# Attention and Fourier mixing on one core: block-diagonal omega and v, the maximum as bias of exp, a shorter weight narrowing, and a list of matmuls that counts other engines

## The chip, the cores and the metric

The kernel runs on one core of one Trainium2 chip. The metric is the device time of one execution in microseconds (us); a median over the runs is quoted. Engines are named as in the profile: PE is TensorE (PEld its weight loads), DVE is VectorE, ACT is ScalarE, POOL is GpSimd, SP is SyncE. The granted clock is the share of TensorE's full clock rate that the profile's records show for a stretch. PSUM is the memory that matmuls write to; a PSUM slot is one of the few buffers there that a matmul group needs before it can start.

## The reference, cut to what matters

```python
# q, k, v: (8, 8, 576, 64), omega: (128, 64), w1: (512, 2048), w2: (2048, 512), float64 weights
def phi(x):                                   # features of keys and of queries (cut: both are first scaled by 64**-0.25)
    proj = einsum('bhsd,md->bhsm', x, omega)
    h = proj - sum(x*x)/2
    h = h - max(h, axis=-1)
    return exp(h) / sqrt(m)
kv  = einsum('bhsm,bhsd->bhmd', k_p, v);  z = sum(k_p, axis=2)
att = (q_p @ kv) / (q_p @ z + 1e-6)           # -> x: (batch 8, 576, 512)
X = fft(fft(x, axis=1), axis=2);  u = x + real(X)          # mixing, one per batch
un = (u - mean) / sqrt(var + 1e-6)
out = u + relu(un @ w1) @ w2                               # the MLP
```

The weights come as 64-bit floats and the chip works in 32 bits, so the kernel narrows both weight matrices itself, with integer operations on the high and low words. A **pair** below is two heads of one batch: four pairs make a batch and there are 32. A batch can be mixed when its four pairs are done. The MLP needs the mixed rows and the narrowed weights. TensorE's matmuls go by the names of their outputs: `tps` and `tp` are transposes, `pp` the features, `kvp` and `ndp` the two products of attention, `yp` and `ab` the two of mixing, `hp` and `op` the two layers of the MLP.

## The kernel before: the parts concerned

Narrowing one part (256 columns): a load, seven operations on VectorE, an addition on GpSimd.

```python
def narrow(dst, src):
    raw = cvt.tile([128, n, 2], U32, name="raw", tag="raw")
    nc.gpsimd.dma_start(raw, src)
    lo, hi = raw[:, :, 0], raw[:, :, 1]
    nc.vector.tensor_scalar(ta[:], hi, 0x7FFFFFFF, None, op0=ALU.bitwise_and)
    nc.vector.tensor_scalar(ta, ta, HI_LOW, HI_HIGH, op0=ALU.max, op1=ALU.min)   # the clamp
    # ... (cut: four more bit operations) ...
    nc.vector.scalar_tensor_tensor(rest[:], lo, 2.0**-52, tb[:].bitcast(F32), ...)
    nc.gpsimd.tensor_tensor(out=dst, in0=ta[:].bitcast(F32), in1=rest[:], op=ALU.add)
```

The features of a pair (`pp`), with both heads in the two halves of the array's rows:

```python
for t in range(3):
    for j in range(3):
        for par in range(2):
            rows = slice(D * par, D * par + D)               # 64 of 128 rows
            nc.tensor.matmul(ps[:, par, MF*j : MF*j+MF], lhsT=kqT[rows, 3*t+j, :], rhs=omT[rows, :])
    nc.vector.tensor_reduce(mx[:], pr4, axis=AX.X, op=ALU.max)
    nc.vector.tensor_tensor(out=e, in0=pr4, in1=mx(broadcast), op=ALU.subtract)
    nc.scalar.activation(out=e[:], in_=e[:], func=AF.Exp, scale=SCALE)
```

Mixing of a batch: three gathers by GpSimd, `half` and `fold` on VectorE and GpSimd, then matmuls `yp` and `ab`.

```python
def mix(b):
    nc.sync.dma_start(x[0:CW, 0:NC3, :], rows[...])              # xs, written by the batch's four pairs
    for c in range(NC3):                                         # NC3 = 3
        nc.gpsimd.indirect_dma_start(out=x[:, NC3 + c, :], in_=rows[:, :], in_offset=turned[:, c])
    yield 0.0, 5.0
    # ... (cut: half and fold, first on VectorE, then on GpSimd) ...
    yield 0.0, 6.0
    for n, tab in enumerate((cs, cs, sn, sn)):
        # ... (cut: yp <- fold, tab; y <- yp) ...
        yield 1.5, (11.0 if n == 1 else 1.0)
```

TensorE's order is made when the program is built: every stream of work (weights, mixing, two of pairs, the MLP) gives, at each `yield`, the time on TensorE of what it has just issued and the time until it can go on, and the loop takes the stream that is ready first. These times are constants in the code; nothing at run time changes the order. The order of the other engines' instructions is settled when the program is built too, around TensorE's; in the trace of the kernel after, the 260 operations and transfers of GpSimd stand in just the built order.

Of the kernel before, what the change touches and what calls it, by code (L numbers as in the profile page):

```python
# [12 lines left out]
AF = mybir.ActivationFunctionType  # L13
# [15 lines left out]


HI_LOW = float(np.uint32(896 << 20).view(np.float32))
# [31 lines left out]
def kernel(  # L63
# [24 lines left out]
    CV = 256  # L88
# [3 lines left out]
    TB = 512  # L92
    NTB = B * S // TB
    SCALE = 1.0 / math.sqrt(math.sqrt(D))
# [6 lines left out]
    ld = ctx.enter_context(tc.tile_pool(name="ld", bufs=2))  # L101
    att = ctx.enter_context(tc.tile_pool(name="att", bufs=2))
    fft = ctx.enter_context(tc.tile_pool(name="fft", bufs=1))
    small = ctx.enter_context(tc.tile_pool(name="small", bufs=4))
    cvt = ctx.enter_context(tc.tile_pool(name="cvt", bufs=2))
# [23 lines left out]

    def load_v(n):  # L130
        b, pr = divmod(n, NP)
        h = slice(2 * pr, 2 * pr + 2)
        v1 = ld.tile([P, R, D + 1], F32, name="v1", tag="v1")
        nc.sync.dma_start(v1[:, :, 0:D], v[b, h].rearrange("i (p r) d -> (i p) r d", r=R))
        nc.gpsimd.memset(v1[:, :, D : D + 1], 1.0)  # L135
        loaded["v", n] = v1

    om = const.tile([128, 2, D], F32, name="om")
    for i in range(2):
        nc.sync.dma_start(om[:, i, :], omega[:, :])  # L140
    for n in range(2):
        load(n)
        load_v(n)
# [26 lines left out]
    def narrow(dst, src):  # L170


        n = dst.shape[1]
        raw = cvt.tile([128, n, 2], U32, name="raw", tag="raw")
        nc.gpsimd.dma_start(raw[:].rearrange("p n two -> p (n two)"), src.bitcast(U32))
        lo, hi = raw[:, :, 0], raw[:, :, 1]
        ta = cvt.tile([128, n], U32, name="ta", tag="ta", bufs=1)
        tb = cvt.tile([128, n], U32, name="tb", tag="tb", bufs=1)

        nc.vector.tensor_scalar(ta[:], hi, 0x7FFFFFFF, None, op0=ALU.bitwise_and)  # L180
        nc.vector.tensor_scalar(
            ta[:].bitcast(F32), ta[:].bitcast(F32), HI_LOW, HI_HIGH, op0=ALU.max, op1=ALU.min
        )

        nc.vector.tensor_scalar(
            ta[:], ta[:], 3, 0x40000000, op0=ALU.logical_shift_left, op1=ALU.bitwise_xor
        )
        nc.vector.tensor_scalar(tb[:], hi, 0x80000000, None, op0=ALU.bitwise_and)
        nc.vector.scalar_tensor_tensor(
            ta[:], ta[:], 0x7FFFFFFF, tb[:], op0=ALU.bitwise_and, op1=ALU.bitwise_or  # L190
        )
        nc.vector.tensor_scalar(tb[:], ta[:], 0xFF800000, None, op0=ALU.bitwise_and)
        rest = cvt.tile([128, n], F32, name="rest", tag="rest", bufs=1)
        nc.vector.scalar_tensor_tensor(  # L194
            rest[:], lo, 2.0**-52, tb[:].bitcast(F32), op0=ALU.mult, op1=ALU.mult
        )
        nc.gpsimd.tensor_tensor(out=dst, in0=ta[:].bitcast(F32), in1=rest[:], op=ALU.add)  # L197
# [4 lines left out]
    def weights():  # L202
        for f in range(0, DFF, CV):
            for j in range(NDC):
                dst, src = w1[:, j, f : f + CV], w1v[:, j, f : f + CV]
                if src.dtype == F32:
                    nc.gpsimd.dma_start(dst, src)
                else:
                    narrow(dst, src)
                    yield 0.0, 3.0  # L210
            there["w1"] = f + CV
        for j in range(NFC):
            for f in range(0, DM, CV):
                dst, src = w2[:, j, f : f + CV], w2v[:, j, f : f + CV]
                if src.dtype == F32:
                    nc.gpsimd.dma_start(dst, src)
                else:
                    narrow(dst, src)
                    yield 0.0, 3.0
            there["w2"] = j + 1  # L220


    omT = const.tile([128, MF], F32, name="omT")
    omps = sml_tile("omps")
    nc.tensor.transpose(omps[:, 0:128], om[:].rearrange("m i d -> m (i d)"), ident[:])
    nc.vector.tensor_copy(out=omT[:], in_=omps[:, 0:128])
# [4 lines left out]

# [23 lines left out]
    def attn(n):  # L255
        b, pr = divmod(n, NP)
        kq, v1 = loaded.pop(n), loaded.pop(("v", n))
# [3 lines left out]
        if n + 2 < B * NP:  # L261
            load(n + 2)
        yield 1.0, 2.2
# [3 lines left out]
        for t in range(3):  # L267
            ps = big_tile("pp")
            for j in range(3):
                for par in range(2):  # L270
                    rows = slice(D * par, D * par + D)
                    nc.tensor.matmul(  # L272
                        ps[:, par, MF * j : MF * j + MF],
                        lhsT=kqT[rows, 3 * t + j, :],
                        rhs=omT[rows, :],
                    )
            pr4 = ps[:, :, 0:384].rearrange("p two (c m) -> p two c m", m=MF)
            mx = small.tile([P, 2, 3], F32, name="mx", tag="mx")
            nc.vector.tensor_reduce(mx[:], pr4, axis=AX.X, op=ALU.max)  # L279
            e = att.tile([P, 6, MF], F32, name="e", tag="e", bufs=6)  # L280
            nc.vector.tensor_tensor(  # L281
                out=e[:].rearrange("p (c two) m -> p two c m", two=2),
                in0=pr4,
                in1=mx[:].unsqueeze(3).to_broadcast([P, 2, 3, MF]),
                op=ALU.subtract,
            )
            nc.scalar.activation(out=e[:], in_=e[:], func=AF.Exp, scale=SCALE)  # L287
            es.append(e)
            if t:
                yield (1.0, 2.5) if t == 1 else (0.7, 2.5)  # L290

        def feature(c):
            return es[c // 6][:, c % 6, :]

        kvp = big_tile("kvp")
        for r in range(R):
            for i in range(2):
                rows = slice(D * i, D * i + D)
                nc.tensor.matmul(  # L299
                    kvp[:, i, 0 : D + 1],  # L300
                    lhsT=feature(r)[rows],
                    rhs=v1[rows, r, :],
                    start=(r == 0),
                    stop=(r == R - 1),
                )
        kv = att.tile([128, 2, D + 1], F32, name="kv", tag="kv")
        nc.vector.tensor_copy(out=kv[:], in_=kvp[:, :, 0 : D + 1])
        if n + 2 < B * NP:
            load_v(n + 2)
        yield 2.3, 0.5  # L310
        qeT = transposed(lambda r: feature(R + r), "qeT")
        yield 1.0, 2.2
# [31 lines left out]
        yield 1.4, 0.0  # L344


    def mix(b):
        NR = 2 * NC3
        x = fft.tile([CP, NR, DM], F32, name="x", tag="x")
# [12 lines left out]
        yield 0.0, 5.0  # L362
# [25 lines left out]
        yield 0.0, 6.0  # L388

        y = fft.tile([128, 4, NK], F32, name="y", tag="y")  # L390
        for n, tab in enumerate((cs, cs, sn, sn)):
            yp = sml_tile("yp")
            for c in range(NC3):
                nc.tensor.matmul(  # L394
                    yp[:, 0:NK],
                    lhsT=fold[:, c, n, :],
                    rhs=tab[:, c, :],
                    start=(c == 0),
                    stop=(c == NC3 - 1),
                )  # L400
            nc.scalar.activation(out=y[:, n, :], in_=yp[:, 0:NK], func=AF.Copy)
            yield 1.5, (11.0 if n == 1 else 1.0)
        for c in range(NC3):

            ab = big_tile("ab")
# [15 lines left out]
            bmp = fft.tile([CP, 3, KD + 1], F32, name="bmp", tag="fold")  # L421
# [11 lines left out]
            for g, (left, right) in enumerate(((mi, pl), (pl, mi))):  # L433
                u = x[:, NC3 * g + c, :]
                nc.gpsimd.tensor_tensor(  # L435
                    out=u[:, 0:KD], in0=u[:, 0:KD], in1=left[:, 0:KD], op=ALU.add
                )
                nc.gpsimd.tensor_tensor(
# [12 lines left out]
            yield 1.4, 2.0  # L451
        done["mix"] = b + 1
# [14 lines left out]
    def prep(j):  # L467
        while done.get("first", 0) < j:
            yield None
        unT = mlpp.tile([128, NDC, TB], F32, name="unT", tag="unT", bufs=1)  # L470
        for i in range(TB // 128):
            t = TB // 128 * j + i
            u = mlpp.tile([P, DM], F32, name="u", tag="u", bufs=2)
            for p, b, s in rows_of(t):
                nc.sync.dma_start(u[p], us[b][s, :])
            st = small.tile([P, 6], F32, name="st", tag="st")
# [9 lines left out]
            yield 0.0, (6.0 if i == 0 else 1.5)  # L486
# [10 lines left out]
            yield 0.5, 0.5  # L497
        uns[j] = unT
        done["prep"] = j + 1
# [4 lines left out]
    def mlp(j):  # L504
        unT = uns.pop(j)
        hs = []
        for fc in range(NFC):
            while there["w1"] < 128 * fc + 128:
                yield None
# [17 lines left out]
            yield 3.45, 0.0  # L527
        for i in range(TB // 128):
            t = TB // 128 * j + i
            ur = mlpp.tile([P, DM], F32, name="ur", tag="ur", bufs=2)  # L530
            for p, b, s in rows_of(t):
                nc.sync.dma_start(ur[p], us[b][s, :])
            yp = mmp.tile([128, DM], F32, name="op", tag="mm")
            for fc in range(NFC):
                while there["w2"] < fc + 1:
                    yield None
                nc.tensor.matmul(  # L537
                    yp[:],
                    lhsT=hs[fc][:, 128 * i : 128 * i + 128],
                    rhs=w2[:, fc, :],  # L540
                    start=(fc == 0),
                    stop=(fc == NFC - 1),
# [80 lines left out]
```

## Time and profile before

The time is 1615.7 us (1611.88 to 1616.73). The profiled span is 1612.1 us.

| | before |
|---|---|
| PE busy | 1430.2 us |
| DVE, ACT, POOL busy | 562.8, 243.2, 304.3 us |
| mean granted clock of TensorE | 0.926 |
| first MLP matmul (`hp`) starts | 187.0 us |
| first gather of mixing issued | 82.8 us |

"Full-clock work" is the sum of TensorE's instructions in the order in which they are listed, each at the rate that it shows in dense stretches at granted clock 1; the prediction shows how the rates are read. "Lost" is the span less that work, and so takes in pauses and time at a lower clock. Before, the work is 1348.8 us and 263.3 are lost: 111.7 by the first `hp` (187.0 us, 75.3 of work listed ahead of it) and 151.6 after it.

### The profile page before, as it was taken

How to read it: one execution, taken by the hardware profiler on the slowest of the kernel's cores; microseconds unless marked ns; L12 is line 12 of the kernel's file. 1: busy time of each engine (PE TensorE's matmuls, PEld its weight loads, DVE VectorE, ACT ScalarE, POOL GpSimd, SP SyncE). 2: the span in 40 equal slices, each digit the busy share in tenths (PEclk: the TensorE clock that was granted, in tenths of full speed). 3: DMA queues.
4: the chain of work that ended last, by engine and by line, in shares of the span. 5: the costliest groups of instructions: out<-in, count | busy, mean ns of one | idle time of the engine just before them, and what ended most of it. 6: DMA issues, size and time to landing. Idle time of an engine off the chain costs nothing.

```text
span 1612.1 us, 17293 instructions
## 1 busy us (share of the span) xinstructions
PE 1430.2 (89%) x7009; PEld 810.2 (50%) x7009; DVE 562.8 (35%) x1269; ACT 243.2 (15%) x389; POOL 304.3 (19%) x387
## 2 busy tenths in 40 slices
PE   6764947865998999799997999899979999999999
PEld 5653626444555566455664555344534544444443
DVE  5778768773323333423423330211111012001000
ACT  2321202122112222122221220000100010000000
POOL 2245344432203002300041000410230020000000
PEclk7765777987998999999998999999989999999999
DMA  5535423342222123312231111202111001001000
GB/s 152 141 93 153 119 64 95 115 119 64 87 69 69 37 83 89 86 37 67 75 101 52 30 47 39 67 7 59 33 40 52 26 30 52 26 5 48 13 12 28
DMA packets 132197, 104.08 MB, mean 65 GB/s; under 512 B 98596, under 2 KB 98852, under 8 KB 132118
## 3 DMA queue, kind: packets, MB, share of 16 engines
q1 hardware_dynamic: 105616, 75.63, 16.6%
q0 software_dynamic: 25856, 26.41, 5.7%
q8 instruction: 55, 0.90, 0.2%
q10 hardware_dynamic: 646, 0.94, 0.2%
q14 instruction: 24, 0.20, 0.0%
HBM read 74.50 MB, written 28.31 MB: 64 GB/s over the span
## 4 chain that ended last, share of the span: by engine, by line
PE 68%; DMA 10%; DVE 7%; POOL 5%; issue 4%; ACT 0%; SPq 0%; POOLq 0%; DVEq 0%; ACTq 0%
PE op L537 29%; PE hp L512 23%; DMA x<-xs,turned 4%; PE kvp L299 3%; PE yp L394 3%; PE tps L242 3%; PE pp L272 3%; POOL x L356 2%; DMA raw<-in_moe_w_ch_dram 2%; DMA us<-x 2%; DMA us<-x,turned 2%; PE ndp L317 1%; PE ab L409 1%; POOL w L197 1%; PE tp L489 1%
## 5 line engine op out<-in xcount | busy, mean ns | idle before, releaser
L512 PE MATMUL hp<-unT,w 128*128 128x512 f32 x1152 | 521.2, 606 | 18.1 <-DVE ht L521 17.6
L537 PE MATMUL op<-w,ht 128*128 128x512 f32 x1152 | 513.0, 596 | 0.0
L512 PEld LDWEIGHTS hp<-unT,w 128*128 128x128 f32 x1152 | 218.1, 194 | 272.9 <-issue 248.0
L537 PEld LDWEIGHTS op<-w,ht 128*128 128x128 f32 x1152 | 213.3, 190 | 241.5 <-issue 235.9
L521 DVE TENSOR_SCALAR ht<-hp 128x512 f32<-128x512 f32 x72 | 49.7, 690 | 306.7 <-PE hp L512 306.7
L272 PE MATMUL pp<-omT,kqT 64*128 64x128 f32 x1152 | 95.6, 311 | 33.6 <-DVE e L281 25.5
L287 ACT ACTIVATE e<-e 128x768 f32<-128x768 f32 x96 | 80.9, 843 | 266.2 <-DVE e L281 264.7
L279 DVE TENSOR_REDUCE mx<-pp 128x6 f32<-128x768 f32 x96 | 91.3, 951 | 65.7 <-PE pp L272 65.7
L272 PEld LDWEIGHTS pp<-omT,kqT 64*128 64x128 f32 x1152 | 81.1, 212 | 64.6 <-issue 51.8
L546 DVE TENSOR_TENSOR ur<-ur,op 128x512 f32<-128x512 f32 x36 | 24.7, 686 | 234.4 <-PE op L537 234.4
L523 ACT ACTIVATE ht<-hp 128x512 f32<-128x512 f32 x72 | 42.9, 596 | 415.1 <-PE hp L512 415.1
L299 PE MATMUL kvp<-v,e 64*128 64x65 f32 x1152 | 89.2, 319 | 11.5 <-DVE e L281 5.5
L299 PEld LDWEIGHTS kvp<-v,e 64*128 64x128 f32 x1152 | 85.1, 232 | 27.2 <-issue 26.8
L281 DVE TENSOR_TENSOR e<-pp,mx 128x768 f32<-128x768 f32 x96 | 91.6, 954 | 4.4 <-DVE mx L279 0.5
L482 POOL TENSOR_TENSOR rstd<-rstd,mhalf 128x1 f32<-128x1 f32 x36 | 20.3, 565 | 356.0 <-DVE rstd L481 355.9
L197 POOL TENSOR_TENSOR w<-ta,rest 128x256 f32<-128x256 f32 x64 | 48.1, 752 | 144.8 <-DVE rest L194 132.3
L394 PE MATMUL yp<-cs_sb,fold 97*128 97x289 f32 x96 | 31.9, 475 | 45.2 <-DVE fold L380 45.2
L435 POOL TENSOR_TENSOR x<-x,bmp 97x257 f32<-97x257 f32 x48 | 33.0, 688 | 164.6 <-DVE bmp L430 164.2
L317 PE MATMUL ndp<-kv,qeT 128*64 128x65 f32 x1152 | 43.3, 233 | 21.4 <-DVE e L281 12.4
L242 PE MATMUL tps<-ident,kq 128*128 128x128 f32 x288 | 45.3, 311 | 18.5 <-issue 12.1
L135 POOL MEMSET v<- 128x9 f32 x32 | 3.6, 114 | 304.3 <-PE kvp L299 240.0
L478 DVE BATCH_NORM_STATS2 st<-u 128x6 f32<-128x512 f32 x36 | 24.8, 690 | 98.7 <-DMA u<-us 98.5
(61 smaller groups left out, 1023.4 us busy)
## 6 DMA issues: line engine op xcount, KB each, us to landing
raw<-in_moe_w_ch_dram POOLq DMA_DIRECT2D x64, 256.0 KB, 3.1
kq<-in_k_dram SPq DMA_DIRECT2D x32, 288.0 KB, 3.1
kq<-in_q_dram SPq DMA_DIRECT2D x32, 288.0 KB, 3.9
v<-in_v_dram SPq DMA_DIRECT2D x32, 288.0 KB, 4.5
xs<-xo SPq DMA_DIRECT2D x64, 144.0 KB, 2.5
out_dram<-ur SPq DMA_DIRECT2D x36, 256.0 KB, 3.2
u<-us SPq DMA_DIRECT2D x32, 256.0 KB, 2.8
ur<-us SPq DMA_DIRECT2D x32, 256.0 KB, 3.2
```

The source lines that it names most:

```text
L197: nc.gpsimd.tensor_tensor(out=dst, in0=ta[:].bitcast(F32), in1=rest[:], op=ALU.add)
L242: nc.tensor.transpose(to[:, 0:128], src(j), ident[:])
L272: nc.tensor.matmul(ps[:, par, MF * j : MF * j + MF], lhsT=kqT[rows, 3 * t + j, :], rhs=omT[rows, :],)
L279: nc.vector.tensor_reduce(mx[:], pr4, axis=AX.X, op=ALU.max)
L281: nc.vector.tensor_tensor(out=e[:].rearrange("p (c two) m -> p two c m", two=2), in0=pr4, in1=mx[:].unsqueeze(3).to_broadcast([P, 2, 3, MF ...
L287: nc.scalar.activation(out=e[:], in_=e[:], func=AF.Exp, scale=SCALE)
L299: nc.tensor.matmul(kvp[:, i, 0 : D + 1], lhsT=feature(r)[rows], rhs=v1[rows, r, :], start=(r == 0), stop=(r == R - 1),)
L317: nc.tensor.matmul(ndp[cols, r // 5, (D + 1) * (r % 5) : (D + 1) * (r % 5 + 1)], lhsT=qeT[:, r, cols], rhs=kv[:, i, :],)
L394: nc.tensor.matmul(yp[:, 0:NK], lhsT=fold[:, c, n, :], rhs=tab[:, c, :], start=(c == 0), stop=(c == NC3 - 1),)
L512: nc.tensor.matmul(hp[:], lhsT=w1[:, dc, 128 * fc : 128 * fc + 128], rhs=unT[:, dc, :], start=(dc == 0), stop=(dc == NDC - 1),)
L521: nc.vector.tensor_scalar(ht[:], hp[:], 0.0, None, op0=ALU.max)
L537: nc.tensor.matmul(yp[:], lhsT=hs[fc][:, 128 * i : 128 * i + 128], rhs=w2[:, fc, :], start=(fc == 0), stop=(fc == NFC - 1),)
```

## The change

The intent: take VectorE off the path at the start, by giving the subtraction of the maximum to ScalarE's exp (as its bias) and by narrowing with four VectorE operations instead of seven; do the two heads of a pair in one matmul each; and list TensorE's work with a model that also counts the other engines and the PSUM slots. The diff, cut to its core:

```diff
-    CV = 256
-    TB = 512
+    CV = 512
+    TB = 384
 def narrow(dst, raw):                                  # raw is loaded two parts ahead
+    nc.gpsimd.tensor_scalar(hif, hif, -HI_HIGH, HI_HIGH, op0=ALU.max, op1=ALU.min)      # L250
+    nc.vector.tensor_scalar(bits, hi, 0x80000000, None, op0=ALU.bitwise_and)            # L251
+    nc.scalar.activation(out=hif, in_=hif, func=AF.Copy, scale=2.0**-112)               # L254
+    nc.vector.scalar_tensor_tensor(bits, hi, 3, bits, logical_shift_left, bitwise_or)   # L255
+    nc.vector.tensor_scalar(hi, bits, 0xFF800000, None, op0=ALU.bitwise_and)            # L258
+    nc.vector.scalar_tensor_tensor(lof, lo, 2.0**-52, hif, op0=ALU.mult, op1=ALU.mult)  # L259
+    nc.gpsimd.tensor_tensor(out=dst, in0=dst, in1=lof, op=ALU.add)                      # L260
-    (seven VectorE operations and the addition)
 def attn(n):
-    for par in range(2): matmul(ps[:, par, ...], lhsT=kqT[rows, 3*t+j, :], rhs=omT[rows, :])
+    matmul(flat_ps[:, 256*j : 256*j+256], lhsT=kqT[:, 4*t+j, :], rhs=om2)   # om2: block-diagonal, scaled
-    nc.vector.tensor_tensor(... op=ALU.subtract); one exp of 768 columns
+    nc.vector.tensor_reduce(nmx, ..., op=ALU.max, negate=True)
+    for c in range(num): nc.scalar.activation(out=e[:, c, :], in_=..., func=AF.Exp, bias=nmx[:, c : c + 1])
-    for i in range(2): matmul(kvp[:, i, 0 : D+1], lhsT=feature(r)[rows], rhs=v1[rows, r, :])
+    matmul(kvp[:, 0 : 2*(D+1)], lhsT=feature(r), rhs=vd[:, r, :])           # vd: block-diagonal
 def mix(b):
+    yield Step(chain=((DMA, 9.0),), when=lambda: done.get(("attn", b), 0) == NP)
     # (gathers)
-    yield 0.0, 5.0
+    yield Step(chain=((DVE, 4.4), (POOL, 8.0)))
-    y = fft.tile(..., tag="y");  bmp = fft.tile(..., tag="fold")
+    y = fft.tile(..., tag="half");  bmp = fft.tile(..., tag="bmp", bufs=2)
 # ... (cut: half of mixing's additions go to VectorE; loads of the norm moved ahead) ...
-    streams = [weights(), mixing(), pairs(0), pairs(1), channels()]        # loop on yields
+    Listing({"big": 2, "sml": 2, "mm": 2}).run([norms(), mixing(), pairs(0), pairs(1), weights(), channels()])
```

A `Step` of the new list gives TensorE time, PSUM slots, and the chain of times on other engines that follows. `Listing` keeps a clock for each engine and takes the step that can begin first.

## The prediction

> **What bounds the kernel now.** I read the page from the top: busy shares, the slices, then the waits of TensorE, then stretches of the span that I cut where the work changes, then single instructions in the timeline.
>
> ```profile
> PE 1430.2 (89%) x7009; PEld 810.2 (50%) x7009; DVE 562.8 (35%) x1269; ACT 243.2 (15%) x389; POOL 304.3 (19%) x387
> DVE  5778768773323333423423330211111012001000
> PEclk7765777987998999999998999999989999999999
> ...
> PE yp L394 <- DVE fold L380: 45.2, 3, 24.7
> PE pp L272 <- DVE e L281: 25.5, 15, 4.2
> PE tp L489 <- DVE u L483: 17.4, 2, 16.5
> ...
> 0.00:190.00 190.00, 124.50 (x1062) 109.32 (x1063) 139.26 (x352) 45.46 (x68) 70.45 (x108) 0.68 0.46 129
> 190.00:413.00 223.00, 154.57 (x1023) 101.59 (x1021) 146.50 (x367) 39.91 (x65) 89.76 (x114) 0.85 0.33 94
> 413.00:1052.00 639.00, 602.80 (x3527) 345.69 (x3528) 205.03 (x397) 121.72 (x191) 97.17 (x110) 0.97 0.23 64
> 1052.00:1612.00 560.00, 548.28 (x1402) 253.56 (x1400) 71.99 (x153) 36.06 (x65) 46.90 (x57) 0.99 0.11 31
> ```
>
> The whole span says "TensorE, 89%", but the slices and the four stretches (columns: length, then busy time of PE, PEld, DVE, ACT, POOL, then granted clock) say two stages. Up to about 413 us, where the weights have just been narrowed, VectorE is busy for 286 us and TensorE waits for it (the three waits named are the largest of TensorE in that stage) and runs at a granted clock of 0.68 and 0.85. After that TensorE is busy 94% and then 98% of the time at nearly full clock: only less TensorE work or fewer gaps can help there.
>
> To size both stages I need TensorE's work at full clock. The timeline gives it, as the distance from one group's start to the next one's:
>
> ```profile
> 572.03 1.15 PE L242 MATMUL tps<-ident,e 128*128 128x128 f32 x9
> 573.01 1.15 PE L242 MATMUL tps<-ident,kq 128*128 128x128 f32 x9
> 577.96 1.27 PE L317 MATMUL ndp<-kv,qeT 128*64 128x65 f32 x36
> 579.16 0.94 PE L272 MATMUL pp<-omT,kqT 64*128 64x128 f32 x12
> 585.70 0.94 PE L272 MATMUL pp<-omT,kqT 64*128 64x128 f32 x12
> 586.57 3.70 PE L537 MATMUL op<-w,ht 128*128 128x512 f32 x8
> 590.20 2.23 PE L299 MATMUL kvp<-v,e 64*128 64x65 f32 x36
> 592.35 3.70 PE L537 MATMUL op<-w,ht 128*128 128x512 f32 x8
> 1498.36 55.10 PE L512 MATMUL hp<-unT,w 128*128 128x512 f32 x128
> 1553.29 55.10 PE L537 MATMUL op<-w,ht 128*128 128x512 f32 x128
> ```
>
> 128 hp instructions take 54.93 us, 429 ns each, 0.84 ns a column. kvp takes 2.15 us per pair of heads (60 ns an instruction), pp 0.87 us per 12 instructions (72.5 ns), ndp 1.20, nine transposes 0.98. I summed these over the order in which the built program issues matmuls: the kernel before holds **1349 us** of full-clock TensorE work (989 of it the two MLP layers). So the span of 1612 loses 263 us. Laying that sum beside the trace: third mixing done at 413 us with 216 us of work issued (197 lost); eighth mixing at 1296 with 1035 issued (63 more lost, in pauses such as 7.65 us before ndp at 671, where VectorE waits for mixing's gather); the last 316 us hold 313 of work.
>
> **What the Trainium skill says.** (1) "TensorE: Matmul & The Clock Gate", Part 1: the array runs at half clock until it has been busy for about 3.4 us. The trace agrees: 72 kvp instructions at granted clock 0.50 take 7.87 us at 29.6 us, 109 ns each, against 60 at clock 1.00. Gaps in the first stage therefore cost twice. (2) "TensorEngine Tiling (Array Packing)", When to Use Tiling: contraction of 64 or less can use two row tiles, up to 2x. The trace gives less: pp at 72.5 ns against the 107 ns that 128 columns cost at hp's rate, 1.5x; kvp at 60 ns against 54 for 65 columns, no gain. (3) "ScalarE: Activation LUTs", What ACT_TABLE_LOAD costs: an ACTIVATE with immediate operands takes 186 ns + 0.833 ns a column, a per-partition bias adds 93 ns, neighbours overlap by 93 ns. The trace has 843 ns for 768 columns (page: 826) and 596 for 512 (612); it has no bias form. (4) "SBUF — State Buffer", Who interferes with whom: VectorE's two-input and two-port operations and GpSimd's share a port pair as an exclusive lock. The trace agrees: a VectorE narrowing step with median 295 ns took 3.33 us when it began under GpSimd's 3.53 us subtraction at 104.5 us.
>
> **The change part by part.**
> - *Block-diagonal omega.* 36 pp instructions of 128 columns per pair become 18 of 256: 18 x 256 x 0.84 = 3.9 us against 36 x 72.5 ns = 2.6. It **adds** 1.3 us x 32 pairs = 41 us to TensorE.
> - *Block-diagonal v.* 36 kvp of 65 columns become 18 of 130: 2.0 us against 2.15, -5 us in all. With MLP tiles of 384 rows (+1 us) TensorE's full-clock work goes to **1386 us**, +37.
> - *Maximum as bias of exp.* VectorE's subtraction goes (96 x 954 ns = 91.6 us). ScalarE's 96 exps of 843 ns become 576 of 128 columns: by the page 280 + 107 - 93 = 0.29 us each, an estimate; 5.3 us a pair, 170 us against 81. With 2.4 us of transposes ScalarE has 7.7 us a pair beside TensorE's 9.1: under it, not by much.
> - *Shorter narrowing.* Before, 64 x 7 VectorE steps took 174 us with their blocking (medians: 5 x 0.29 + 2 x 0.425 = 2.3 us per 256 columns). After, 32 x 4 steps on 512 columns. From 0.29 and 0.425 at 256, with a fixed 0.16: 2 x 0.42 + 2 x 0.69 = 2.2 us, 71 us. GpSimd gets a clamp (guess 0.7 us) and the addition (1.28 us, on the line through 1003 and 3452 ns for 384 and 1536 columns): 64 us against 48. ScalarE gets 32 x 0.6.
> - *Half of mixing's additions from GpSimd to VectorE:* +24 us there over the span, off the path later.
> - *The list.* It sets the matmul order. In the built order 94 us of TensorE work stand before the end of pair 8, about where the MLP starts; by then VectorE's order holds nearly all narrowing. After each batch's attention the list leaves 26 to 53 us of other matmuls before mixing needs its gather (13 for the first batch). Before, a gather's round took 19 us (three issues of 2.2, then 11.9). So I expect the pauses after 413 us, 63 us, to fall to some 15.
>
> **The sum.** VectorE's work up to pair 8: narrowing 71, 8.5 pairs x 4.55 (maxima 2 x 1.22 + 0.42, the rest 1.7) = 39, one mixing 12, first normalisation 5: **127 us**. But the port is shared: VectorE's port steps (79 us) and GpSimd's (64 + 12 of mixing) can't overlap: **155 us**. At 90% use, after an 8 us start: pair 8 ends at about **180 us** (before: 190 us, but with 80 us of TensorE work issued, and a weight stage still to 356 us). From there 1386 - 94 = 1292 us of TensorE work, 15 of pauses, 3 for the last addition and store: 1490. The run is 3.7 us over the profiled span: 1494; I lean a little to a better overlapped start and say **1488 us**, 8% less.
>
> **Rivals.**
> (a) *The start stays bound.* The new narrowing hops GpSimd, ScalarE, VectorE, VectorE, GpSimd, each in a strict queue; ScalarE's copy stands behind eight exps. For it: the coupled order on all queues and the 24.5 us that VectorE already waits before narrowing's first step up to 190 us. Against: three buffers with two parts ahead. It would put pair 8 at 220 us: 1530.
> (b) *ScalarE becomes the bound of attention*, if an exp costs 0.37 us without overlap: 9.1 us a pair, TensorE's own figure. Early only, since later pairs are paced between MLP work: 1510.
> (c) *TensorE's extra 37 us eats the gain*, if the pauses after 413 us remain 63: 1540. Against: their cause, the tile that waits for its own batch's mixing, is decoupled in the list.
> (d) *Everything overlaps*: the first stage runs at VectorE's 127 us and full clock: 1440.
>
> **Range and chances.** The middle is the sum; (d) gives the low end, (a) or (c) the high end, both at once 1580. Slower than 1583 needs a wait that I have not seen: **1488**, range **1445 to 1535**; faster by over 2% 0.95, same 0.04, slower 0.01.
>
> **What would show it.** pp rows of 128x256 at about 215 ns an instruction (right) or well below; kvp 576 instructions near 111 ns. VectorE busy near 400 us, ScalarE near 350. Narrowing's four VectorE groups under 95 us together and finished by about 185 us. First hp near 150 to 185 us. PE busy near 1420 us, mean clock above 0.926. TensorE pauses after the MLP starts at 15 us in sum, none of over 5 us on mixing. The prediction is wrong if the first hp stands after 215 us, if exps are dense on ScalarE while TensorE waits, or if TensorE waits on mixing past 250 us.

## The result and the profile after

The changed kernel takes **1620.7 us** (median, 1618.99 to 1622.72), beside 1615.7 for the kernel before. The ratio is 1.0036, with a 95% interval of 1.0014 to 1.0057: no gain, and 133 us above the prediction. Ratios here are the mean time of one kernel's fast runs over that of the other's fast runs in the same rounds, so not quite the ratio of the medians quoted.

The page's busy shares and two of its rows by slice (VectorE, TensorE's granted clock), then its rows for the clamp, the exps, pp and kvp; columns are busy time, mean duration of one, idle time before them and its cause:

```profile
PE 1449.6 (90%) x6241; PEld 905.3 (56%) x6241; DVE 456.9 (28%) x926; ACT 339.3 (21%) x925; POOL 324.8 (20%) x282
...
DVE  3675763331312323132232323122110101010010
...
PEclk9776768998999999899989999998999999999999
...
L360 ACT ACTIVATE e<-pp,nmx 128x128 f32<-128x128 f32 x576 | 154.4, 405 | 182.0 <-DVE nmx L351 181.9
L345 PE MATMUL pp<-om,kqT 128*128 128x256 f32 x576 | 142.3, 399 | 18.2 <-ACT e L360 10.2
...
L374 PE MATMUL kvp<-vd,e 128*128 128x130 f32 x576 | 78.2, 295 | 6.5 <-ACT e L360 6.5
L250 POOL TENSOR_SCALAR raw<-raw 128x512 f32<-128x512 f32 x32 | 67.7, 2117 | 49.2 <-DMA raw<-in_moe_w_ch_dram 49.0
```

VectorE did lose over 100 us and the clock did rise, to 0.942. But its slices 3 to 6 (81 to 243 us) still read 7, 5, 7 and 6, and one clamp takes GpSimd 2.1 us in the mean. The stretches of the span, cut at the first `hp` (columns: length, busy time of PE, PEld, DVE, ACT, POOL, clock, DMA share, GB/s), show where that falls. Before, then after:

```profile
0.00:187.00 187.00, 121.50 (x1056) 107.99 (x1056) 137.03 (x345) 44.40 (x67) 69.12 (x106) 0.67 0.46 130
```

```profile
0.00:234.00 234.00, 124.27 (x763) 104.05 (x764) 145.54 (x237) 86.43 (x235) 155.17 (x129) 0.76 0.50 142
```

Up to the first `hp`, GpSimd is now the busiest engine of all, with 155 us in place of 69, and VectorE stands idle for 88 of 234 us: VectorE's throughput does not bound this stage, yet the stage is 47 us longer. The waits of VectorE in the first 130 us of the kernel after (total, times, longest) say why:

```profile
DVE w L251 <- POOL raw L250: 34.8, 17, 7.8
```

Its first narrowing operation waits for GpSimd's clamp, and VectorE's later instructions, the maxima among them, stand behind it in its order. The timeline of GpSimd just ahead of the first gather (start, duration, and in brackets the idle time before it with its cause) shows the second half of the matter:

```profile
117.66 2.19 POOL L250 TENSOR_SCALAR raw<-raw 128x512 f32<-128x512 f32 x1 [1.41 <-DMA raw<-in_moe_w_ch_dram]
119.80 1.29 POOL L260 TENSOR_TENSOR w<-w,raw 128x512 f32<-128x512 f32 x1
121.39 0.59 POOL L279 DMA_DIRECT2D raw<-in_moe_w_ch_dram  x1 [0.30 <-POOL w L260]
126.73 2.14 POOL L250 TENSOR_SCALAR raw<-raw 128x512 f32<-128x512 f32 x1 [4.75 <-DMA raw<-in_moe_w_ch_dram]
129.07 2.44 POOL L433 DMA_INDIRECT x<-xs,turned  x1 [0.20 <-issue]
```

Each part is a loop through one queue: issue the load, wait for it to land, clamp, add. Here the clamp waits 4.75 us for its part, and the gather, which has nothing to do with weights, comes after it. In the order as built 20 clamps and 17 additions stand ahead of the first gather; before, 13 additions and no clamp. In the trace of the kernel after, the 260 operations and transfers of GpSimd stand in just the built order. The first gather is issued at 129.1 us in place of 82.8, and the first `hp` comes at 234.1 in place of 187.0: the same 46 to 47 us. Most of that delay is older than GpSimd's last clamp, though: the store of the first batch's fourth pair, which the gather needs, is issued at 117.9 us in place of 78.5, so 39 of the 46 us are there before it, and 7 come between store and gather.

The second place is at the later mixings. The waits of TensorE, after:

```profile
PE yp L471 <- DVE fold L457: 31.3, 6, 16.1
PE yp L471 <- ACT y L478: 24.4, 5, 6.7
PE tp L573 <- DVE rstd L564: 18.0, 1, 18.0
PE ndp L394 <- DVE kv L382: 14.0, 2, 9.4
```

`yp` is mixing's first matmul, and 11 times TensorE stands waiting for it: 23 us in sum at the first mixing, which is still ahead of the first `hp`, and 6 to 8 us at each of five of the seven others. One such mixing, from the chain of work that ended last (start, duration):

```profile
644.65 1.22 PE ndp L394 x36
...
651.70 2.26 POOL x L433
...
654.26 2.18 POOL x L433
...
656.74 13.27 DMA x<-xs,turned
...
675.52 3.44 POOL half L448
...
680.92 1.96 POOL fold L457 x2
...
683.62 5.78 PE yp L471 x12
```

From the end of the batch's last `ndp` (645.9 us) to the rows landing (670.0) 24 us pass: 4.5 to store `xs`, then 19.6 from the gathers' turn to their landing. Then `half` and `fold` on VectorE and GpSimd take 13 more, to 683.1: 37 us in all. The list reckons 4.5 for the store, 9.0 for the gather, 12.4 for `half` and `fold`, 26 in sum, and so in the order as built the full-clock work from that `ndp` to `yp` is 25.5 us in the steady state. TensorE loses 11.9 us at this mixing: it waits 7.3, and its 24 `yp` take 10.6 us at a granted clock of 0.65, where those of the last mixing take 6.0 at full clock.

The balance, in the measure above:

| | before | predicted | after |
|---|---|---|---|
| full-clock work | 1348.8 | 1386 | 1386.0 |
| lost by the first `hp` | 111.7 | 86 | 148.5 |
| lost after it | 151.6 | 18 | 82.7 |
| span | 1612.1 | 1490 | 1617.2 |

(The predicted column is the prediction's own sum: pair 8 at 180 us less 94 of work, then 15 of pauses and 3 at the end, before it rounded to 1488.) The change gained 69 us after the first `hp`, lost 37 before it, and added 37 of work.

### The profile page after: what moved, and what is told of

Read it like the earlier page. It is cut to its first block, busy times and chain, and to the rows that moved or that the text cites. A ratio compares the mean times of both kernels' runs of the same rounds, so it can differ in the third digit from the quotient of the medians.

```text
span 1617.2 us, 15802 instructions
## 1 busy us (share of the span) xinstructions
PE 1449.6 (90%) x6241; PEld 905.3 (56%) x6241; DVE 456.9 (28%) x926; ACT 339.3 (21%) x925; POOL 324.8 (20%) x282
## 4 chain that ended last, share of the span: by engine, by line
PE 71%; DMA 12%; POOL 9%; DVE 4%; issue 3%; ACT 1%; SPq 0%; POOLq 0%; DVEq 0%; ACTq 0%
PE hp L601 30%; PE op L633 24%; DMA x<-xs,turned 7%; PE pp L345 4%; DMA raw<-in_moe_w_ch_dram 3%; PE kvp L374 3%; PE tps L310 3%; PE yp L471 3%; POOL raw L250 2%; POOL x L433 2%; PE ndp L394 2%; POOL w L260 1%; PE ab L488 1%; DMA xs<-xo 1%; DVE nmx L351 1%
## 5 line engine op out<-in xcount | busy, mean ns | idle before, releaser
L601 PE MATMUL hp<-unT,w 128*128 128x384 f32 x1536 | 514.5, 491 | 8.7 <-DVE ht L610 8.7
L601 PEld LDWEIGHTS hp<-unT,w 128*128 128x128 f32 x1536 | 291.5, 192 | 204.4 <-issue 10.7
L360 ACT ACTIVATE e<-pp,nmx 128x128 f32<-128x128 f32 x576 | 154.4, 405 | 182.0 <-DVE nmx L351 181.9
L345 PE MATMUL pp<-om,kqT 128*128 128x256 f32 x576 | 142.3, 399 | 18.2 <-ACT e L360 10.2
L610 DVE TENSOR_SCALAR ht<-hp 128x384 f32<-128x384 f32 x96 | 53.5, 557 | 356.8 <-PE hp L601 356.8
L345 PEld LDWEIGHTS pp<-om,kqT 128*128 128x128 f32 x576 | 114.1, 202 | 43.7 <-ACT e L360 11.1
L351 DVE TENSOR_REDUCE nmx<-pp 128x8 f32<-128x1024 f32 (+1 forms) x96 | 89.6, 951 | 97.4 <-PE pp L345 97.0
L374 PEld LDWEIGHTS kvp<-vd,e 128*128 128x128 f32 x576 | 76.9, 209 | 14.8 <-ACT e L360 7.6
L374 PE MATMUL kvp<-vd,e 128*128 128x130 f32 x576 | 78.2, 295 | 6.5 <-ACT e L360 6.5
L250 POOL TENSOR_SCALAR raw<-raw 128x512 f32<-128x512 f32 x32 | 67.7, 2117 | 49.2 <-DMA raw<-in_moe_w_ch_dram 49.0
L471 PE MATMUL yp<-cs_sb,fold 97*128 97x289 f32 x96 | 36.2, 540 | 34.5 <-DVE fold L457 31.3
L310 PE MATMUL tps<-ident,kq 128*128 128x128 f32 x288 | 43.7, 303 | 24.2 <-issue 11.2
```

What stands on the lines that cost most here:

```text
L250: nc.gpsimd.tensor_scalar(hif, hif, -HI_HIGH, HI_HIGH, op0=ALU.max, op1=ALU.min)
L310: nc.tensor.transpose(to[:, 0:128], src(j), ident[:])
L345: nc.tensor.matmul(flat_ps[:, 256 * j : 256 * j + 256], lhsT=kqT[:, 4 * t + j, :], rhs=om2[:].rearrange("p i m -> p (i m)"),)
L351: nc.vector.tensor_reduce(nmx[:], flat_ps[:, 0 : MF * num].rearrange("p (c m) -> p c m", m=MF), axis=AX.X, op=ALU.max, negate=True,)
L360: nc.scalar.activation(out=e[:, c, :], in_=flat_ps[:, MF * c : MF * c + MF], func=AF.Exp, bias=nmx[:, c : c + 1],)
L374: nc.tensor.matmul(kvp[:, 0 : 2 * (D + 1)], lhsT=feature(r), rhs=vd[:, r, :], start=(r == 0), stop=(r == R - 1),)
```

## The experiments

Twelve kernels were run, each compared with the reference; all are correct but one. Each was timed beside the kernel before in its own call; the kernel before had medians of 1613.9 to 1615.7 us in the four calls, so differences between runs of different calls are good to about 2 us. In the expectations that name theories by a letter, L is the theory that the list leaves too little work before mixing, and C that the chain of the first batch sets the start. "Pair 4" is when the last store of the last of the first batch's four pairs is issued, "first gather" when GpSimd issues it. All in us.

| run | median | ratio to before (95%) | pair 4 | first gather | first hp | work | lost by first hp | lost after |
|---|---|---|---|---|---|---|---|---|
| before | 1615.7 | 1 | 78.5 | 82.8 | 187.0 | 1348.8 | 111.7 | 151.6 |
| after | 1620.7 | 1.0036 (1.0014 to 1.0057) | 117.9 | 129.1 | 234.1 | 1386.0 | 148.5 | 82.7 |
| a_clamp_dve | 1586.4 | 0.9824 (0.98 to 0.9849) | 95.5 | 102.0 | 197.1 | 1386.0 | 111.5 | 86.2 |
| a_no_narrow | 1573.5 | 0.9743 (0.9718 to 0.9767) | 98.0 | 101.6 | 184.1 | 1386.0 | 98.5 | 86.8 |
| a_row_omega | 1586.2 | 0.9827 (0.9797 to 0.9856) | 92.2 | 110.2 | 208.1 | 1349.6 | 140.2 | 95.1 |
| a_gather20 | 1571.8 | 0.9726 (0.9699 to 0.9753) | 116.2 | 128.6 | 235.0 | 1386.0 | 142.2 | 42.3 |
| a_bufs_old | 1610.1 | 0.9968 (0.9944 to 0.9993) | 117.4 | 129.6 | 231.8 | 1386.0 | 146.2 | 78.4 |
| a_gather20_bufs | 1574.9 | 0.9753 (0.9729 to 0.9777) | 115.6 | 127.5 | 235.8 | 1386.0 | 143.0 | 42.4 |
| b_narrow | 1655.7 | 1.0255 (1.0229 to 1.028) | 81.0 | 90.0 | 197.6 | 1348.8 | 122.3 | 181.6 |
| b_narrow_dve | 1625.2 | 1.0055 (1.0038 to 1.0072) | 81.7 | 88.0 | 186.5 | 1348.8 | 111.2 | 163.8 |
| b_bias | 1619.4 | 1.0039 (1.0001 to 1.0078) | 82.4 | 90.0 | 189.3 | 1348.8 | 114.0 | 147.6 |
| a_first4 | 1592.1 | 0.985 (0.9834 to 0.9865) | 93.9 | 107.6 | 192.1 | 1386.0 | 116.2 | 88.9 |
| a_three | 1522.4 | 0.9424 (0.9411 to 0.9437) | 81.4 | 88.7 | 181.5 | 1349.6 | 104.1 | 66.9 |
| a_three_first4 | 1510.8 | 0.9349 (0.9337 to 0.9362) | 80.8 | 88.8 | 182.7 | 1349.6 | 105.3 | 57.4 |

Names with a_ start from the kernel after, with b_ from the kernel before.

### The clamp on VectorE (a_clamp_dve)

```diff
-        nc.gpsimd.tensor_scalar(hif, hif, -HI_HIGH, HI_HIGH, op0=ALU.max, op1=ALU.min)
+        nc.vector.tensor_scalar(hif, hif, -HI_HIGH, HI_HIGH, op0=ALU.max, op1=ALU.min)
```

> The changed kernel with one line altered: narrowing's clamp runs on VectorE in place of GpSimd. Theory G (GpSimd's queue bounds the start: per part it holds a clamp of 2.0 us, an addition of 1.3, an issue of 0.6 and the wait for its own transfer): GpSimd loses 68 us of work, VectorE gets 32 x 0.42 = 13 us, the first hp moves from 234 us to 170-195 us and the run falls by 35 to 60 us, to 1560-1585. Rival V (VectorE and the port it shares, or attention's own chain, bound the start whatever the engine of the clamp): first hp stays at 225-240 us, the time within 10 us of 1620.

It is 34 us faster than the kernel after, all of it ahead of the first `hp` (lost 111.5 in place of 148.5; after it 86.2 in place of 82.7). Theory G's ranges were missed by a hair (197.1 and 1586.4 us for up to 195 and 1585), the rival's by far. The fourth pair is stored 22 us earlier, and the gather follows 6.5 us later in place of 11.2. Giving VectorE more work made the kernel faster. The same instruction on the two engines, from the source line's view (minimum, median and maximum in ns), first in the kernel after, then in this run:

```profile
L250 POOL TENSOR_SCALAR raw<-raw x32: 1953/2008/3167, 11.9 to 228.9; 128x512 f32<-128x512 f32 x32
```

```profile
L250 DVE TENSOR_SCALAR raw<-raw x32: 396/428/1781, 12.8 to 202.4; 128x512 f32<-128x512 f32 x32
```

### No narrowing at all (a_no_narrow)

Of the narrowing only one VectorE operation stays, so the weights are wrong (relative error 0.40).

```diff
-        nc.gpsimd.tensor_scalar(hif, ...)           # clamp
         nc.vector.tensor_scalar(bits, hi, 0x80000000, None, op0=ALU.bitwise_and)
-        nc.scalar.activation(...); two nc.vector.scalar_tensor_tensor; one nc.vector.tensor_scalar
-        nc.gpsimd.tensor_tensor(out=dst, ...)       # addition
```

> Wrong result on purpose: the weights are still fetched, but narrowing is one VectorE operation a part (weights become zeros), with no clamp, no copy and no addition. Floor of the start. If narrowing as a whole bounds it: first hp at 120-150 us, the run falls by 85 to 110 us, to 1510-1535. Rival C (attention's own chain of maxima, exps and PSUM slots bounds it): first hp still after 190 us and the run falls by under 45 us.

Without the work of narrowing the kernel after is 47 us faster. Even so the first `hp` starts at 184.1 us, and not far earlier, as a stage bound by VectorE's throughput would have it. Both theories' ranges were missed: 184.1 lies well after the 150 of the one and just ahead of the 190 of the other, and 47 us is near the other's 45. The engines' busy time up to 187 us (columns as before) shows how little VectorE has left to do there:

```profile
0.00:187.00 187.00, 116.45 (x768) 96.78 (x769) 65.01 (x148) 67.70 (x205) 44.45 (x67) 0.83 0.60 178
```

VectorE is busy for 65.0 us, where it was 137.0 before. The run is not a strict floor: the one operation left still waits for each part's load, 34 us in sum in the first 118. What remains is a chain of the first batch: its four pairs are done at 97 us, the gathers go out at 101.6, `yp` starts at 126, `ab` ends at 148, the transposes of the normalised rows start at 172. In all fourteen kernels the first `hp` comes 82 to 108 us after the first gather.

### The maximum as bias, alone in the kernel before (b_bias)

```diff
-            nc.vector.tensor_tensor(out=e, in0=pr4, in1=mx(broadcast), op=ALU.subtract)
-            nc.scalar.activation(out=e[:], in_=e[:], func=AF.Exp, scale=SCALE)
+            for c in range(3):
+                for par in range(2):
+                    nc.scalar.activation(out=e[:, 2*c+par, :], in_=ps[:, par, MF*c : MF*c+MF],
+                                         func=AF.Exp, bias=mx[:, par, c : c+1])
```

(The maximum is taken with its sign turned, and the scale goes into omega.)

> The kernel before with the maximum as bias of exp alone (scale folded into omega, six exps of 128 columns per group). Prediction's step: VectorE loses 96 x 954 ns = 92 us, half of it in the start that it bounds, ScalarE gains 576 x 0.27 - 81 = 75 us; the run falls by 15 to 45 us, to 1570-1600. Rival: ScalarE's six exps take longer (6 x 0.27 = 1.6 us) than subtraction and one exp did on two engines in a pipeline, pp's slots come free no earlier, and the time stays within 12 us of before.

VectorE's busy time falls by 79 us (562.8 to 484.2), the first `hp` stays (189.3 us), and so does the time. The waits of TensorE in this run:

```profile
PE pp L272 <- ACT e L283: 14.4, 8, 4.0
PE ndp L318 <- ACT e L283: 12.4, 2, 10.2
PE tps L242 <- ACT e L283: 9.5, 2, 8.9
```

In the kernel before, the same matmuls waited on VectorE's `e` (25.5 and 12.4 us, the first of them shown in the prediction). The wait changed its name and kept most of its length. A relief of VectorE by 79 us over the run was worth nothing by itself. At the start there was hardly any relief: up to 187 us VectorE is busy for 134.0 us in place of 137.0, since narrowing of 36 parts begins there in place of 31.

### The shorter narrowing, alone in the kernel before (b_narrow), and with its clamp on VectorE (b_narrow_dve)

The edit of b_narrow is the new `narrow` of the diff above, on parts of 256 columns and loaded as before. b_narrow_dve differs from it by one word:

```diff
-        nc.gpsimd.tensor_scalar(hif, hif, -HI_HIGH, HI_HIGH, op0=ALU.max, op1=ALU.min)
+        nc.vector.tensor_scalar(hif, hif, -HI_HIGH, HI_HIGH, op0=ALU.max, op1=ALU.min)
```

> The kernel before with the shorter narrowing alone, on its own 256-column parts and in its own order. Theory G (GpSimd's strided clamp, 3.9 ns a column, makes the shorter narrowing no cheaper): clamp 64 x 1.05 us, GpSimd busy up by 67 us, VectorE down by 50 to 70 us; the time within 20 us of before, slower as likely as faster. Rival (the saving of VectorE's work is what counts, as the prediction had it): the start shortens by 40 us or more, the run to 1575 or less.

> The kernel before with the shorter narrowing, and its clamp on VectorE in place of GpSimd (with the clamp on GpSimd this was 1655.7 us, 41 slower). If the engine of the clamp was the whole of that loss, the time is that of before or below it, 1590 to 1616 us: VectorE has two operations fewer a part than before. If the loss lay in the longer round trip VectorE, ScalarE, VectorE, GpSimd itself, it stays at 1640 to 1656 us.

The shorter narrowing alone makes the kernel before 41 us **slower**, outside the ranges of both theories (theory G had allowed 20); 11 of them are lost by the first `hp` and 30 after it. GpSimd's busy time rises by 75 us, and VectorE's falls by 38, not by 50 to 70. The waits of VectorE in b_narrow hold the reason:

```profile
DVE w L180 <- POOL raw L179: 103.7, 41, 16.0
```

With the clamp on VectorE, 30 of the 41 us are gone. So the engine of the clamp was most of that loss. Ten stay, though the part now has five VectorE operations in place of seven: the expectation that it would be level or faster missed. In the kernel before, VectorE's narrowing waits 58 us in sum (for loads and for GpSimd's addition); in b_narrow_dve it is 92, of which 67.7 are for loads and 24.1 for ScalarE's copy, which stands between two of its operations. The hop to ScalarE and back is thus the likely cause of the ten, but no run takes it away alone.

### Row halves for omega (a_row_omega)

```diff
+                if num == 8:                       # 16 of the 18 blocks of a pair
+                    for par in range(2):
+                        nc.tensor.matmul(ps[:, par, MF*j : MF*j+MF],
+                                         lhsT=kqT[half, 4*t+j, :], rhs=om2[half, par, :])
+                    continue
-                0.22 * num,
+                0.145 * num if num == 8 else 0.22 * num,
```

> The changed kernel with omega's row halves brought back for 16 of the 18 feature blocks of a pair (two matmuls of 64 rows and 128 columns in two banks, in place of one of 128 rows and 256 columns); the maximum stays a bias. If block-diagonal omega costs TensorE 1.3 us a pair on the path, as the prediction worked out: pp goes from 3.9 to 2.75 us a pair at full clock, 32 x 1.15 = 37 us, and the run falls by 25 to 40 us, to 1580-1595. Rival: attention lies in stretches where TensorE waits for others, so a shorter pp is idle time: the run falls by under 12 us.

The work falls by 36.4 us and the time by 34.5. The price that the prediction put on block-diagonal omega, 41 us for all 18 blocks, stands as far as TensorE's work goes. That the time fell by nearly as much is in part luck, for the pair's shorter constant also shifts the list: the fourth pair is stored 26 us earlier, four clamps fewer come ahead of the first gather, and the first `hp` is 26 us earlier; the first `hp` also has 18 us less work listed ahead of it, so only 8 us of loss went there, and 12 came back later. PE busy is 1401.1 us in place of 1449.6.

### The list's constants for mixing (a_gather20), and the buffers (a_bufs_old, a_gather20_bufs)

```diff
-        yield Step(chain=((DMA, 9.0),), when=lambda: done.get(("attn", b), 0) == NP)
+        yield Step(chain=((DMA, 20.0),), when=lambda: done.get(("attn", b), 0) == NP)
-        yield Step(chain=((DVE, 4.4), (POOL, 8.0)))
+        yield Step(chain=((DVE, 5.0), (POOL, 8.0)))
```

No instruction is added or removed, only the order changes. The rival: in the kernel after, `y` shares its buffer with GpSimd's `half`, so the wait might come from that. Its test:

```diff
-        y = fft.tile([128, 4, NK], F32, name="y", tag="half")
+        y = fft.tile([128, 4, NK], F32, name="y", tag="y")
-            bmp = fft.tile([CP, 3, KD + 1], F32, name="bmp", tag="bmp", bufs=2)
+            bmp = fft.tile([CP, 3, KD + 1], F32, name="bmp", tag="fold")
```

> The changed kernel with two constants of its list altered: the gather of a mixing is put at 20 us in place of 9 and VectorE's fold at 5.0 in place of 4.4. In the trace of the changed kernel xs landed at 650.4 us and the gather at 670.0, 19.6 us, so mixing's matmuls stand about 11 us too early in TensorE's order. Theory L: TensorE's waits of yp on VectorE's fold and on ScalarE's y (31.3 and 24.4 us) nearly vanish after 240 us, the 80 us that TensorE loses between first hp and eighth mixing fall to 10-35, and the run falls by 45 to 70 us, to 1550-1575. Rival: the matmuls that move ahead have no PSUM slot or no data either, or the next step (the second product, the store, the next tile) takes the wait over: the run falls by under 20 us.

> The changed kernel with mixing's buffers as before: y in a buffer of its own, bmp in fold's buffer. Theory B (y shares half's buffer, so the first evictions of y wait for GpSimd's half of the folding, and TensorE's third and fourth yp wait for them): TensorE's waits of yp on ACT y (24.4 us) go to under 5 us, lost TensorE time per mixing falls from about 11 us to 5-6, the run falls by 25 to 45 us, to 1575-1595. Rival L (the gather comes later than the list assumes, so TensorE waits there anyway): sn's yp then wait for GpSimd's fold directly, the wait only changes its name, and the run stays within 10 us of 1620.

> The same list constants, and mixing's buffers as before (y in its own buffer, bmp in fold's). If the gather was the whole wait, this is within 8 us of the list constants alone; if y waiting for GpSimd's half of the folding is a wait of its own, it is faster than them by a further 10 to 25 us.

Two constants are worth 49 us, as theory L had it. In the order as built 36 to 38 us of full-clock work now stand ahead of `yp` from the third mixing on, in place of 25.5, and after the first `hp` TensorE waits for `yp` for 2.3 us in sum. The loss after the first `hp` halves, from 82.7 to 42.3, and that before it hardly moves. The largest waits of TensorE with them; the two rows of `yp` that led the list in the kernel after are not among them:

```profile
PE tps L310 <- ACT e L360: 30.9, 5, 18.0
PE tp L573 <- DVE rstd L564: 18.7, 1, 18.7
PE ndp L394 <- DVE kv L382: 17.8, 3, 9.7
PE pp L345 <- ACT e L360: 14.6, 3, 9.4
```

The buffers alone gave 10.6 us at most, and with the constants nothing (1574.9 against 1571.8). With the buffers alone the wait of `yp` stayed, at 32.8 us on VectorE's `fold` and 9.4 on GpSimd's: the rival falls as the main cause.

### The first batch's pairs first (a_first4)

```diff
         for n in range(first, B * NP, 2):
+            if n >= NP:
+                yield Step(when=lambda: done.get(("attn", 0), 0) == NP)
```

> The changed kernel with only the order of the first eight pairs changed (the first batch's four pairs alone first). Latency chain: first hp at 215 to 222 us in place of 234, total 1605 to 1620 us, as later pauses are untouched. Throughput: first hp at 230 us or later, total 1621 us or more.

The first `hp` comes at 192.1 us, 42 earlier, and the total falls by 29: more than the chain's theory had asked for (its ranges were missed on the good side). In the order as built, 16 clamps and 14 additions now stand ahead of the first gather, instead of 20 and 17, and the gather goes out at 107.6. So part of what I had called a chain of the first batch is GpSimd's order again: parts of weights that were listed while the second batch's pairs were worked on had been standing in front of the first batch's gather. Not all of it, as the fourth pair itself is stored earlier too, at 93.9 us in place of 117.9; this run does not separate the two.

### All three, and with the first batch first (a_three, a_three_first4)

The edits of a_clamp_dve, a_row_omega and a_gather20 together; the second adds that of a_first4.

> The changed kernel with the three edits that each gained alone: the narrowing's clamp on VectorE (gained 34 us), the row halves kept for 16 of the 18 omega blocks (34.5 us), and the list told 20 us for mixing's gather and 5.0 us for the fold (49 us). If the three causes are separate places in the run (start, TensorE's own work, pauses at mixing), the gains add: 1621 - 34 - 34.5 - 49 = about 1503 us, and the lost time of TensorE falls from 231 us to about 150. If they are partly one cause (an earlier start is eaten by the next wait, or shorter omega work gives mixing less work to hide behind), they overlap and the time is 1520 to 1545 us. Either way it should beat both kernels.

> The same three edits, and pairs of the second batch are kept out of the list until the first batch's four pairs are listed. Theory of a latency chain (the first MLP work comes when the first batch's four pairs, the gather, the fold, yp and the norm have followed one another): the first hp comes 12 to 20 us earlier than in the run without this edit, and the total falls by up to that much, 1485 to 1500 us. Theory of throughput at the start (VectorE or the narrowing of all eight pairs sets it): the first hp stays or comes at most 5 us earlier and the total is the same or longer, since TensorE then idles where the second stream's pairs filled in.

a_three takes 1522.4 us, 5.8% less than before and 98 less than the kernel after. The sum of the single gains would be 118. Adding the single changes of the two columns of loss gives 97 and 58 us, and 104.1 and 66.9 came: so 7 of the missing 20 are lost by the first `hp` and 9 after it (the rest is the difference between medians and profiled executions). Why is not shown. It is not mixing: `yp` does not wait at all in this run. The wait of `hp` for VectorE's `ht` stands out, 25.2 us in place of 8.7 in the kernel after, and it is 24.1 in a_row_omega, which alone lost 12 us more after the first `hp` too. The fourth edit gives a further 11.6 us, but not where it was expected: the first `hp` stays (182.7 us against 181.5), since the gather was already issued at 88.7, with 12 additions ahead of it and no clamp, and the gain lies after it (57.4 us lost). The fourth pair was already stored at 81.4 us without the edit (80.8 with it), so there was nothing left for this order to bring forward. This version, **1510.8 us**, beats both kernels; the page's busy shares of it:

```profile
PE 1386.7 (92%) x6753; PEld 854.5 (57%) x6753; DVE 452.9 (30%) x958; ACT 338.4 (22%) x925; POOL 259.5 (17%) x250
```

## Why the prediction was wrong, point by point

**Right.** The full-clock work and its cost: a group of eight pp starts 1.73 us before the next one and 18 kvp take 2.02 us, which is 216 and 112 ns an instruction (said: 215 and 111); taking back 8/9 of block-diagonal omega took 36.4 us out of the work, where 41 implies 36. The exp as bias: eight exps take 2.17 us, 0.27 each, where 0.29 was estimated; ScalarE's 339 us were put at 350, and rival (b), a bound by ScalarE, did not come (its 0.37 us without overlap should have been 280 + 107 = 387 ns by the page's own figures). With mixing's wait gone, though, the wait for ScalarE's exps leads TensorE's list: 30.9 us at `tps` in a_gather20, 29.2 at `kvp` in a_three_first4. The timeline of the kernel after that carries these numbers:

```profile
484.45 1.89 PE L345 MATMUL pp<-om,kqT 128*128 128x256 f32 x8
486.18 1.04 PE L573 MATMUL tp<-ident,u 128*128 128x128 f32 x8
...
496.52 2.18 PE L374 MATMUL kvp<-vd,e 128*128 128x130 f32 x18
498.54 1.15 PE L310 MATMUL tps<-ident,e 128*128 128x128 f32 x9
```

```profile
490.31 2.17 ACT L360 ACTIVATE e<-pp,nmx 128x128 f32<-128x128 f32 x8 [0.35 <-DVE nmx L351]
```

**Wrong, first step: "VectorE is busy for 286 us and TensorE waits for it".** I took a busy engine on which TensorE waits for the bound of the stage, and made the new start of 180 us out of its throughput. a_no_narrow contradicts this: it takes nearly all narrowing away, VectorE is busy for 65.0 of the first 187 us, and the first `hp` is still at 184.1. (b_bias proves less: its 79 us hardly fall in the start.) What sets the start is when the first gather is issued, which needs the first batch's four pairs and GpSimd's turn, and the chain behind it, 82 to 108 us long in every run. Where the gather came 27 and 22 us earlier, in a_clamp_dve and a_first4, the first `hp` came 37 and 42 us earlier. The wait that the profile puts down to VectorE was the last link of that chain, and another engine took its place when it was relieved.

**Wrong, second step: the clamp on GpSimd, "guess 0.7 us".** It took 2.0 us (median), so GpSimd's narrowing cost 32 x (2.12 + 1.34, the means of clamp and addition) = 111 us and not 64. The size is not the whole error. The step treated GpSimd's time as load on a shared port; it is also an order. A clamp that waits 4.75 us for its part holds the gather behind it, and VectorE's narrowing waits for clamps (34.8 us in the first 130), with the maxima of attention behind it. Rival (a) had described strict queues ("hops GpSimd, ScalarE, VectorE, VectorE, GpSimd, each in a strict queue") and was set aside by "three buffers with two parts ahead"; its 220 us was the nearest to the 234.1 that came. Measured: 34 us for the clamp's engine in the kernel after, 30 in the kernel before. VectorE's narrowing came to 108 us (the means of its four operations, 938, 947, 733 and 752 ns, by 32), not 71: of their medians, 662, 693, 420 and 682, the sum would be 79.

**Wrong, third step: "the list leaves 26 to 53 us of other matmuls before mixing needs its gather", so pauses of 15 us.** The 19 us of a gather's round were read off in the prediction and never set against the list's own 9.0, nor were the store and the 13 us of `half` and `fold` added. And the slack was misread: the pair that completes a batch is the later of the two streams', which leaves 25.5 us in the steady state, not 53. The need is 24 + 13 = 37 us. The shortfall of 11 to 12 us is what the mixing shown lost (11.9, of which 7.3 are waiting), and a_gather20 got back 49 us by giving the list a constant near the measured one.

**The sum.** Of the 127 us between 1490 and the span, 62 are lost by the first `hp` and 65 after it, none in the work. The runs got a part of each back: moving the clamp 37 of the 62, the list's two constants 40 of the 65. Some 25 on either side are not accounted for by them. The range's upper end combined neither: the prediction named (a) and (c) together as 1580 and gave that little chance, although both rest on one habit of this kernel, an order fixed by constants, and even 1580 falls 40 short.

**What stays open.** The gain of 69 us after the first `hp` belongs to the new list and the earlier loads by exclusion: b_bias and b_narrow do not show it, but no run has the new list alone in the kernel before. b_narrow_dve's last 10 us are argued, not shown. Why the fourth pair is stored at 98.0 us in a_no_narrow, with no clamp or addition left, where the kernel before has it at 78.5, was not followed up: in the order as built the fourth pair now ends together with the fifth, and VectorE still waits for loads of weights, and no run tells these apart. And the prediction's 155 us for VectorE and GpSimd on a shared port was tested by no run.

## What to carry to other kernels

An engine that is busy and waited for is not yet the bound of a stage: take its work away in one run, and see whether the stage ends earlier, before a prediction is built on its throughput. When an operation moves to another engine, ask what stands behind it in that engine's order, above all when it waits for a transfer. A list that orders matmuls by constants is only as good as those constants: measure each chain, from the last matmul that feeds it to the first one that needs it, and set the number beside the constant.

## What the Trainium skill lacked or had wrong

- "GPSIMD Engine Reference", Engine selection and Performance pitfalls for Q7 kernels: the first calls GpSimd's one-input operations roughly line-rate, the second puts a cost of about 1.9 cycles an element up to a byte step of 8 and 2.9 above it. The clamp here has one input, two operations, 32-bit elements at a step of 8 bytes, in place: 2008 ns for 512 columns (median), 3.9 ns a column, where VectorE took 428 ns. For 256 columns it took 1102 ns. The page's figure, 1.9 cycles at the clock of 1.2 GHz that it uses, would give an estimate of 0.8 us; it is stated for programs on GpSimd's own cores, so it may not be meant for this instruction. The measurement decides, and a row for such an operation is lacking.
- "DMA: Bandwidth & Descriptors", Anatomy of one DMA — SWDGE (gpsimd) path: the fit, 2.0 us plus bytes over 436 KB a us, gives an estimate of 2.5 us for the 97 rows of 2 KB that one gather brings. It has no figure for an indirect transfer. The chain shows 2.2 us of issue for each of three, and 13.27 us from the third one's issue to its landing.
